# Attention and a two-layer block on one core: the second part of q moves to GpSimd, the factor 0.125 into the exponential, and first-layer units alternate with second-layer units

## The chip, the cores and the metric

The kernel runs on one core of a Trainium2 chip. The metric is the time of one execution on the device, in microseconds (us); less is better. The engines named below are TensorE (PE in the profile: matmuls; PEld: its weight loads), VectorE (DVE), ScalarE (ACT), GpSimd (POOL) and SyncE (SP), which issues the DMAs. PSUM is where TensorE writes. Here it has eight banks in use: four for scores (two buffers of two), three that the two layers share, and one for attention times v.

## The reference

```python
# q, k, v: (8, 8, 576, 64); w_in: (512, 2048); w_out: (2048, 512); all float32
scores = (1.0 / np.sqrt(64)) * np.matmul(q, k.transpose(0, 1, 3, 2))
thresh = np.max(scores, axis=-1, keepdims=True) - tau
scores = np.where(scores >= thresh, scores, -1000000000.0)
scores = scores - np.max(scores, axis=-1, keepdims=True)
attn = np.exp(scores)
attn = attn / (np.sum(attn, axis=-1, keepdims=True) + 1e-09)
x = np.matmul(attn, v)            # then heads side by side: (4608, 512)
h = x @ w_in
g = h * (1.0 / (1.0 + np.exp(-h)))
out = (g @ w_out).astype(np.float32)
```

Every row of scores is cut at its maximum less `tau` (0.02) before the softmax. So small errors in a score decide whether an entry counts, and scores need more accuracy than one rounded product gives.

## The kernel before, in words

**Attention.** Work goes in tiles of 128 rows of scores: 288 tiles in all. Batch 0 is passed twice, first in four "low" visits (16 tiles, rows 0 to 255, computed directly in float32) and then in four "high" ones. Each later batch has four visits of a pair of heads, nine tiles each, so 36 tiles to a batch. For one tile, `scores` multiplies q by k into one of two PSUM buffers (L412). To be accurate, k is split into a rounded part `khi` and a rest `klo` (`split_k`), and q is stacked as a rounded part above its rest in `qstack` (`split_q`), so that two matmuls per half give the whole sum. Then follow the row maximum on VectorE (`soft1`, L422, negated), the threshold on VectorE (L425, maximum less tau), the exponential on ScalarE (`soft1b`, L432, with the negated maximum as its bias), the cut and the row sum on VectorE (`soft2`, L441; it reads the scores again and so frees their buffer), the reciprocal (L445, L449), the scaling on ScalarE (`soft2b`, L454), and the split into two float16 parts on GpSimd (`soft3`, L465, L468, L471). Those are transposed by DMA (L481) and multiplied by v (`av`, L496), two heads at once. `av_post` writes x in two float16 parts (L514, L515).

**q and 0.125.** In batch 0 `split_q` first scales q by `gate` (0.125, or 0 where tau is negative) on ScalarE (L309), rounds it into `qstack` (L310), and GpSimd subtracts to get the rest (L311). From batch 1 on, ScalarE scales and rounds in one step (L315), and VectorE makes the rest, scaling again (L316). `scale_direct` (L349) scales q for the low visits.

**The two layers.** x is taken in chunks of 256 and 320 columns for batch 0 and of 288 for the others, two chunks to a batch. A first-layer unit (`h_unit`, 16 to a chunk) is 12 matmuls into one bank (L530), followed by a chain: tanh on ScalarE (L538), a product on VectorE (L539), the rounded float16 part on ScalarE (L546), its rest on VectorE (L547), into a ring `gbuf` of 17 places. A second-layer unit (`o_unit`) is a quarter of one of four output tiles, 12 matmuls (L562); after the fourth quarter ScalarE evacuates the bank (L572) and SyncE writes it out. `moe_units` gives the 16 first-layer units of a chunk and then its 16 second-layer units. The three banks are handed out in turn by `bank`.

**Weights.** They arrive as 64-bit words. GpSimd, VectorE and ScalarE decode and split them during batch 0 (lines 168 to 214).

**What sets the order.** The program text runs one loop over tiles and drops units between them, at a rate that lets a batch's units end with the next batch. The text's order is a priority only. A scheduler, which reorders the instructions when the program is built, then sets a fixed order for each engine, with scores 1600 places ahead and the steps of the softmax and of `av` ahead by other offsets. On the chip each engine takes its instructions in that order.

## Time and profile before

| | |
|---|---|
| time, three runs | 1277.15, 1279.8 (median), 1281.62 us |
| span of the profiled execution, first to last instruction | 1276.2 us |
| mean granted TensorE clock | 0.969 |
| TensorE busy | 1152.4 us (90%), 9400 matmuls |
| VectorE busy | 967.7 us (76%) |
| ScalarE busy | 819.6 us (64%) |
| GpSimd busy | 751.1 us (59%) |
| chain that ended last | PE 52%, DVE 25%, ACT 6%, DMA 5%, issue 5%, POOL 5% |

The profile gives the span of the profiled execution and no other time of it; the median of the runs is 3.6 us longer than that span. In a row that groups instructions stand the line, the engine, the operation, the tiles it writes and reads, their shapes and the count; then the busy time in us and the mean duration in ns; then the idle time of the engine just before them and what ended it. Tile names stand without their numbers. The rows of stretches of time give for each engine its busy us and, in brackets, its instructions, then the granted clock, the busy share of the DMA engines, and GB/s.

### The profile page before, as it was taken

The numbers are of one execution on the slowest core, as the hardware profiler recorded it, in microseconds if no ns is written. First come the engines' busy times: TensorE is split into PE (matmuls) and PEld (weight loads), VectorE is DVE, ScalarE is ACT, GpSimd is POOL, SyncE is SP. The second block draws the span as 40 slices with busy tenths as digits, with TensorE's granted clock in tenths as the row PEclk, the third lists the DMA queues.
The fourth block names the chain that finished last, engine by engine and source line by source line (L and its number), as shares of the span: only waits on it lengthen the run. The fifth ranks groups of instructions, "written<-read, shape, count | busy, mean of one in ns | idle before, by whom it ended". The sixth has DMA issues, their size and how long they took to land.

```text
span 1276.2 us, 27018 instructions
## 1 busy us (share of the span) xinstructions
PE 1152.4 (90%) x9400; PEld 898.8 (70%) x9400; DVE 967.7 (76%) x2627; ACT 819.6 (64%) x1505; POOL 751.1 (59%) x952
## 2 busy tenths in 40 slices
PE   5774768898899998998989999998999999999998
PEld 3453657676678776776767777786777777777777
DVE  7899998987988989888688858977598848521431
ACT  5787776765867867777476747866477746532431
POOL 4568977787678777874568608781478508300000
PEclk8886989998999999999989999999999999999999
DMA  9457768688778787873768538781687418300000
GB/s 301 121 183 179 172 119 163 138 151 168 135 151 154 135 168 161 156 146 79 152 122 157 114 85 158 148 156 39 129 159 144 103 24 140 72 15 18 8 15 19
DMA packets 363480, 158.15 MB, mean 124 GB/s; under 512 B 329552, under 2 KB 338256, under 8 KB 363344
## 3 DMA queue, kind: packets, MB, share of 16 engines
q1 hardware_dynamic: 363344, 156.43, 59.0%
q8 instruction: 74, 1.21, 0.4%
q14 instruction: 62, 0.51, 0.1%
HBM read 66.72 MB, written 9.44 MB: 60 GB/s over the span
## 4 chain that ended last, share of the span: by engine, by line
PE 52%; DVE 25%; ACT 6%; DMA 5%; issue 5%; POOL 5%; SPq 1%; POOLq 0%; ACTq 0%; DVEq 0%
PE o L562 22%; PE h L530 15%; PE a L496 7%; PE s L412 7%; DVE w L441 6%; DVE sm L422 5%; DVE qstack L316 4%; DMA wT<-hl 3%; ACT w L432 2%; DVE h L539 2%; DVE gbuf L547 2%; POOL hl L468 1%; DMA vraw<-in_vL 1%; ACT w L454 1%; POOL hl L465 1%
## 5 line engine op out<-in xcount | busy, mean ns | idle before, releaser
L530 PE MATMUL h<-x,wst 128*128 128x288 f16 (+2 forms) x3072 | 416.9, 291 | 23.1 <-DVE gbuf L547 19.4
L562 PE MATMUL o<-gbuf,wst 128*128 128x288 f16 (+2 forms) x3072 | 397.3, 287 | 2.5 <-DVE gbuf L547 1.4
L530 PEld LDWEIGHTS <-wst 128*128 128x128 f16 x3072 | 295.0, 99 | 114.9 <-issue 32.0
L562 PEld LDWEIGHTS <-wst 128*128 128x128 f16 x3072 | 291.9, 98 | 85.5 <-issue 8.3
L468 POOL TENSOR_TENSOR hl<-w,hl 128x512 f16<-128x512 f32 x272 | 328.1, 1206 | 15.9 <-ACT hl L463 2.1
L465 POOL TENSOR_SCALAR hl<-w 128x576 f16<-128x576 f32 x264 | 181.5, 690 | 236.6 <-ACT w L454 133.0
L432 ACT ACTIVATE w<-s,sm 128x576 f32<-128x576 f32 x288 | 211.2, 738 | 106.5 <-DVE sm L422 32.2
L441 DVE SCALAR_TENSOR_TENSOR w<-s,sm,w 128x576 f32<-128x576 f32 x288 | 232.7, 812 | 51.1 <-ACT w L432 49.1
L454 ACT ACTIVATE w<-w,sm 128x576 f32<-128x576 f32 x288 | 219.5, 772 | 68.7 <-DVE sm L449 59.5
L422 DVE TENSOR_REDUCE sm<-s 128x1 f32<-128x576 f32 x288 | 216.0, 751 | 55.4 <-PE s L412 51.8
L412 PE MATMUL s<-khi,qstack 128*128 128x288 f32 x608 | 158.7, 342 | 37.2 <-DVE w L441 29.9
L539 DVE SCALAR_TENSOR_TENSOR h<-th,h 128x288 f32<-128x288 f32 (+2 forms) x256 | 116.6, 456 | 80.9 <-ACT th L538 75.8
L538 ACT ACTIVATE th<-h,msc 128x288 f32<-128x288 f32 (+2 forms) x256 | 127.1, 500 | 30.7 <-PE h L530 27.7
L496 PE MATMUL a<-wT,v 128*64 128x288 f16 (+1 forms) x1680 | 131.8, 297 | 14.4 <-DMA wT<-hl 14.1
L546 ACT ACTIVATE gbuf<-h 128x288 f16<-128x288 f32 (+2 forms) x256 | 104.0, 408 | 63.5 <-DVE h L539 62.9
L547 DVE SCALAR_TENSOR_TENSOR gbuf<-h,gbuf 128x288 f16<-128x288 f32 (+2 forms) x256 | 115.0, 452 | 37.9 <-ACT gbuf L546 36.4
L412 PEld LDWEIGHTS s<-khi,qstack 128*128 128x128 f32 x608 | 96.8, 194 | 64.3 <-issue 39.7
L412 PE MATMUL s<-klo,qstack 128*128 128x288 f32 x608 | 133.1, 300 | 0.0
L326 POOL TENSOR_TENSOR klo<-kraw,khi 128x576 fp32r<-128x576 f32 x64 | 93.0, 1453 | 53.9 <-ACT khi L324 52.4
L496 PEld LDWEIGHTS <-v 128*64 128x64 f16 x1680 | 93.7, 112 | 42.1 <-issue 33.3
L412 PEld LDWEIGHTS s<-klo,qstack 128*128 128x128 f32 x608 | 100.2, 193 | 1.0 <-issue 0.2
L471 POOL TENSOR_TENSOR hl<-w,hl 128x64 f16<-128x64 f32 x272 | 94.0, 345 | 0.0
(84 smaller groups left out, 876.5 us busy)
## 6 DMA issues: line engine op xcount, KB each, us to landing
qraw<-in_qT SPq DMA_DIRECT2D x128, 144.0 KB, 3.0
kraw<-in_kT SPq DMA_DIRECT2D x128, 144.0 KB, 3.0
vraw<-in_vL SPq DMA_DIRECT2D x32, 320.0 KB, 3.8
wraw<-in_w_out SPq DMA_DIRECT2D x16, 512.0 KB, 3.9
out_t<-wst SPq DMA_DIRECT2D x56, 144.0 KB, 2.4
wT<-hl SPq DMA_TRANSPOSE x304, 3.4
gbuf<-in_w_in SPq DMA_DIRECT2D x8, 512.0 KB, 7.9
wraw<-in_w_in SPq DMA_DIRECT2D x8, 512.0 KB, 5.4
```

The source lines that it names most:

```text
L412: nc.tensor.matmul(s_ps[:, j, :HALF], lhs, kk[:, j * HALF : (j + 1) * HALF], start=(n == 0), stop=(n == len(seq) - 1),)
L422: nc.vector.tensor_reduce(out=negm, in_=s_ps[:, :, :HALF], op=ALU.max, axis=AX.XY, negate=True)
L432: nc.scalar.activation(wtile[t].rearrange("p (j c) -> p j c", j=2), sps[t][:, :, :HALF], AF.Exp, bias=small[t][:, 0:1],)
L441: nc.vector.scalar_tensor_tensor(out=w3, in0=s_ps[:, :, :HALF], scalar=sm[:, 1:2], in1=w3, op0=ALU.is_ge, op1=ALU.mult, accum_out=sm[:, 2:3],)
L454: nc.scalar.activation(w, w, AF.Copy, scale=r)
L465: nc.gpsimd.tensor_scalar(out=fl[:, 0:S], in0=w, scalar1=1.0, scalar2=1.0, op0=ALU.mult, op1=ALU.mult)
L468: nc.gpsimd.tensor_tensor(out=fl[:, 640:1152], in0=w[:, 0:512], in1=fl[:, 0:512], op=ALU.subtract)
L496: nc.tensor.matmul(a_ps[odd * D : (odd + 1) * D, :n], vt[:, lo_v, odd, kv, :], wT[v, b * H + 2 * p + odd][:, kw, c0 - base : c0 - base + n ...
L530: nc.tensor.matmul(ph[:, :n], wi(c, f, lo_w), x16[b, lo_x][:, c, c0 : c0 + n], start=(k == 0), stop=(k == 11),)
L539: nc.vector.scalar_tensor_tensor(out=ph[:, :n], in0=th[:, :n], scalar=1.0, in1=ph[:, :n], op0=ALU.add, op1=ALU.mult,)
L547: nc.vector.scalar_tensor_tensor(out=g[:, 1, :n], in0=ph[:, :n], scalar=2.0**-14, in1=g[:, 0, :n], op0=ALU.mult, op1=ALU.subtract,)
L562: nc.tensor.matmul(ps[:, :n], wo(f, d, lo_w), g[:, lo_g, :n], start=(f == 0 and k == 0), stop=(f == NF - 1 and k == 2),)
```

## The change

There are three edits. First, q is no longer scaled: ScalarE only rounds it, GpSimd makes the rest for all heads, and `scale_direct` is gone. The factor goes into the exponential as its scale. The exponential's bias must then be the negated maximum times `gate`, and the threshold is the maximum less eight times tau. Both come from one VectorE instruction on two columns, with the constants `cmul` (gate, -1) and `cadd` (0, -8 tau). Second, from batch 1 on the first-layer units of a chunk alternate with the second-layer units of the chunk before it, and the last chunk's second-layer units come at the end. Third, as this needs two whole chunks of g, `gbuf` is larger and addressed by chunk, paid for with a smaller scratch space for DMA descriptors; the first layer takes banks 0 and 1, the second layer bank 2.

```diff
@@ constants
-GB = 17
+GWORDS = 2 * NF * S
@@ def attention_moe
-    gbuf = const.tile([P, GB * 2 * WID], F16, name="gbuf")
+    gbuf = const.tile([P, GWORDS], F16, name="gbuf")
-    gate = const.tile([P, 1], F32, name="gate")
+    cmul = const.tile([P, 2], F32, name="cmul")
+    nc.vector.memset(cmul, -1.0)
+    gate = cmul[:, 0:1]
...
+    cadd = const.tile([P, 2], F32, name="cadd")
+    nc.vector.memset(cadd, 0.0)
...
-        out=ntau, in0=tau_sb, scalar1=0.0, scalar2=-1.0, op0=ALU.max, op1=ALU.mult
+        out=ntau, in0=tau_sb, scalar1=0.0, scalar2=-8.0, op0=ALU.max, op1=ALU.mult
     )
+    nc.vector.tensor_tensor(out=cadd[:, 1:2], in0=ntau, in1=ungated, op=ALU.add)
@@ def pow2_scales
-            allp = bank([P, P], f"{name}_ps")
+            allp = bank([P, P], f"{name}_ps", 0 if turn[1] == 3 else None)
@@ def split_q
-        if h < H:
-            nc.scalar.activation(src, src, AF.Copy, scale=gate)
-            nc.scalar.activation(dst, src, AF.Copy)
-            nc.gpsimd.tensor_tensor(
-                out=dst[D:P, :], in0=src[D:P, :], in1=dst[D:P, :].bitcast(F32), op=ALU.subtract
-            )
-        else:
-            nc.scalar.activation(dst, src, AF.Copy, scale=gate)
-            nc.vector.scalar_tensor_tensor(
-                out=dst[D:P, :], in0=src[D:P, :], scalar=gate[D:P, :],
-                in1=dst[D:P, :].bitcast(F32), op0=ALU.mult, op1=ALU.subtract,
-            )
+        nc.scalar.activation(dst, src, AF.Copy)
+        nc.gpsimd.tensor_tensor(
+            out=dst[D:P, :], in0=src[D:P, :], in1=dst[D:P, :].bitcast(F32), op=ALU.subtract
+        )
@@ def soft1, soft1b
-        nc.vector.tensor_scalar(
-            out=sm[:, 1:2], in0=negm, scalar1=-1.0, scalar2=ntau, op0=ALU.mult, op1=ALU.add
+        nc.vector.scalar_tensor_tensor(
+            out=sm[:, 1:3], in0=cmul, scalar=negm, in1=cadd, op0=ALU.mult, op1=ALU.add
         )
...
-            bias=small[t][:, 0:1],
+            bias=small[t][:, 1:2], scale=gate,
@@ the two layers
+    def place_g(b, c0, n):
+        if gnext[0] + 2 * NF * n > GWORDS:
+            gnext[0] = 0
+        gbase[b, c0] = gnext[0]
+        gnext[0] += 2 * NF * n
...
+    def h_units(b, c0, n, owns=(None,)):
+        return [
+            lambda f=f: h_unit(b, c0, n, f, owns[f % len(owns)]) for f in range(NF)
+        ]
+
+    def o_units(b, c0, n, own=None):
+        return [
+            lambda d=d, quarter=quarter: o_unit(b, c0, n, d, quarter, own)
+            for d in range(DM // P) for quarter in range(4)
+        ]
+
+    held = []
+
     def moe_units(b, c0, n):
-        for f in range(NF):
-            yield lambda f=f: h_unit(b, c0, n, f)
-        for d in range(DM // P):
-            for quarter in range(4):
-                yield lambda d=d, quarter=quarter: o_unit(b, c0, n, d, quarter)
+        if b == 0:
+            return h_units(b, c0, n) + o_units(b, c0, n)
+        out = []
+        if held:
+            for pair in zip(h_units(b, c0, n, (0, 1)), o_units(*held.pop(), 2)):
+                out.extend(pair)
+        else:
+            out = h_units(b, c0, n)
+        held.append((b, c0, n))
+        return out
@@ the loop over tiles
+        if held and not ready and not units and t >= NT + 8:
+            units.extend(o_units(*held.pop()))
@@ def kernel
-    nc = bacc.Bacc("TRN2", target_bir_lowering=False, num_devices=1)
+    nc = bacc.Bacc(
+        "TRN2", target_bir_lowering=False, num_devices=1, dynamic_dma_scratch_size=1024
+    )
```

Since a scheduler decides the order, here is what it made of both programs at three places. Names carry their numbers: `s_192` are the scores of tile slot 192, `h_3_288_1` is first-layer unit 1 of the chunk of batch 3 that begins at column 288, `o_3_0_1` is output tile 1 of the chunk at column 0, and a last number is the buffer's. The changed kernel's lines are a few lower or higher than before: L422, L425, L441, L445, L539, L547 are now L418, L421, L437, L441, L544, L551.

VectorE around tile 192, before:

```order
L422 TENSOR_REDUCE sm_193_9891<-s_193_9843 128x1
L449 RECIPROCAL sm_191_9774<-sm_191_9774 128x1
L316 SCALAR_TENSOR_TENSOR qstack1_87<-qraw_24_41_9855,gate_79,qstack1_87 64x576
L425 TENSOR_SCALAR sm_192_9839<-sm_192_9839,ntau_81 128x1
L547 SCALAR_TENSOR_TENSOR gbuf_61<-h_3_0_9_8459,gbuf_61 128x288
L425 TENSOR_SCALAR sm_193_9891<-sm_193_9891,ntau_81 128x1
L547 SCALAR_TENSOR_TENSOR gbuf_61<-h_3_0_10_8496,gbuf_61 128x288
L441 SCALAR_TENSOR_TENSOR w32_192_9840,sm_192_9839<-s_192_9778,sm_192_9839,w32_192_9840 128x576
```

and of the change:

```order
L418 TENSOR_REDUCE sm_192_9578<-s_192_9528 128x1
L551 SCALAR_TENSOR_TENSOR gbuf_61<-h_3_288_1_9029,gbuf_61 128x288
L421 SCALAR_TENSOR_TENSOR sm_191_9524<-cmul_79,sm_191_9524,cadd_82 128x2
L421 SCALAR_TENSOR_TENSOR sm_192_9578<-cmul_79,sm_192_9578,cadd_82 128x2
L437 SCALAR_TENSOR_TENSOR w32_191_9525,sm_191_9524<-s_191_9472,sm_191_9524,w32_191_9525 128x576
L437 SCALAR_TENSOR_TENSOR w32_192_9579,sm_192_9578<-s_192_9528,sm_192_9578,w32_192_9579 128x576
L441 TENSOR_SCALAR sm_191_9524<-sm_191_9524 128x1
L544 SCALAR_TENSOR_TENSOR h_3_288_2_9084<-th_3_288_2_9125,h_3_288_2_9084 128x288
```

The rest of q (L316) has left VectorE's row. The two small instructions of a pair of tiles still stand between the reduces and the cuts, but they are two-tensor instructions now and follow one another.

GpSimd at the head that is loaded for the same place, before:

```order
L471 TENSOR_TENSOR hl_189_9732<-w32_189_9663,hl_189_9732 128x64
L326 TENSOR_TENSOR klo_41_9941<-kraw_24_41_9856,khi_41_9939 128x576
L465 TENSOR_SCALAR hl_190_9785<-w32_190_9722 128x576
L468 TENSOR_TENSOR hl_190_9785<-w32_190_9722,hl_190_9785 128x512
L471 TENSOR_TENSOR hl_190_9785<-w32_190_9722,hl_190_9785 128x64
```

and of the change:

```order
L461 TENSOR_SCALAR hl_190_9535<-w32_190_9469 128x576
L327 TENSOR_TENSOR klo_41_9701<-kraw_24_41_9595,khi_41_9699 128x576
L318 TENSOR_TENSOR qstack1_93<-qraw_24_41_9594,qstack1_93 64x576
L464 TENSOR_TENSOR hl_190_9535<-w32_190_9469,hl_190_9535 128x512
L467 TENSOR_TENSOR hl_190_9535<-w32_190_9469,hl_190_9535 128x64
```

The rest of q stands right behind the rest of k, ahead of the two float16 subtractions of tile 190.

TensorE where one first-layer unit ends, before:

```order
L530 MATMUL h_2_288_7_7311<-x16_2_1_4317,wst_89 128x288
L530 LDWEIGHTS wst_89
L530 MATMUL h_2_288_7_7311<-x16_2_0_4316,wst_89 128x288
L530 LDWEIGHTS wst_89
L530 MATMUL h_2_288_8_7332<-x16_2_0_4316,wst_89 128x288
```

and of the change:

```order
L535 MATMUL h_3_288_7_9435<-x16_3_1_6164,wst_95 128x288
L535 LDWEIGHTS wst_95
L535 MATMUL h_3_288_7_9435<-x16_3_0_6163,wst_95 128x288
L566 LDWEIGHTS wst_95
L566 MATMUL o_3_0_1_9221<-gbuf_61,wst_95 128x288
```

Unit 7 was followed by unit 8; now it is followed by twelve matmuls of the second layer and then by unit 8.

More of the change, by code (lines that the diff above doesn't have):

```diff
@@ L90, in attention_moe @@
     )
+    cadd = const.tile([P, 2], F32, name="cadd")
+    nc.vector.memset(cadd, 0.0)
+    ungated = const.tile([P, 1], F32, name="ungated")
+    nc.vector.tensor_scalar(
+        out=ungated, in0=tau_sb, scalar1=0.0, scalar2=-3.0e38, op0=ALU.is_lt, op1=ALU.mult
+    )
     ntau = const.tile([P, 1], F32, name="ntau")
     nc.vector.tensor_scalar(
-        out=ntau, in0=tau_sb, scalar1=0.0, scalar2=-1.0, op0=ALU.max, op1=ALU.mult
+        out=ntau, in0=tau_sb, scalar1=0.0, scalar2=-8.0, op0=ALU.max, op1=ALU.mult
     )
+    nc.vector.tensor_tensor(out=cadd[:, 1:2], in0=ntau, in1=ungated, op=ALU.add)
     qstack = []
@@ L344, in load_direct @@
         direct[v] = qt, kt
-    def scale_direct(v):
-        for j in range(2):
-            own = direct[v][0][j * D : (j + 1) * D, 256 * j : 256 * (j + 1)]
-            nc.scalar.activation(own, own, AF.Copy, scale=gate[j * D : (j + 1) * D, :])
     def soft3_direct(t):
@@ L418, in soft1 @@
         s_ps = sps[t]
-        sm = sb.tile([P, 5], F32, tag="small", name=f"sm_{t}", bufs=4)
+        sm = sb.tile([P, 6], F32, tag="small", name=f"sm_{t}", bufs=4)
         w = sb.tile([P, S], F32, tag="w32", name=f"w32_{t}", bufs=4)
@@ L441, in soft2 @@
         nc.vector.scalar_tensor_tensor(
-            out=w3, in0=s_ps[:, :, :HALF], scalar=sm[:, 1:2], in1=w3,
-            op0=ALU.is_ge, op1=ALU.mult, accum_out=sm[:, 2:3],
+            out=w3, in0=s_ps[:, :, :HALF], scalar=sm[:, 2:3], in1=w3,
+            op0=ALU.is_ge, op1=ALU.mult, accum_out=sm[:, 3:4],
         )
         nc.vector.tensor_scalar(
-            out=sm[:, 3:4], in0=sm[:, 2:3], scalar1=1e-9, scalar2=2.0**-12,
+            out=sm[:, 4:5], in0=sm[:, 3:4], scalar1=1e-9, scalar2=2.0**-12,
             op0=ALU.add, op1=ALU.mult,
         )
-        nc.vector.reciprocal(out=sm[:, 4:5], in_=sm[:, 3:4])
+        nc.vector.reciprocal(out=sm[:, 5:6], in_=sm[:, 4:5])
     def soft2b(t):
         w = wtile[t]
-        r = small.pop(t)[:, 4:5]
+        r = small.pop(t)[:, 5:6]
         nc.scalar.activation(w, w, AF.Copy, scale=r)
@@ L521, in attention_moe, with h_unit @@
     gt = {}
-    gcount = [0]
+    gbase = {}
+    gnext = [0]
     po = {}
-    def h_unit(b, c0, n, f):
-        ph = bank([P, 512], f"h_{b}_{c0}_{f}")
+    def place_g(b, c0, n):
[3 more added lines that the diff above has]
+        gnext[0] += 2 * NF * n
+    def h_unit(b, c0, n, f, own=None):
+        if f == 0:
+            place_g(b, c0, n)
+        ph = bank([P, 512], f"h_{b}_{c0}_{f}", own)
         k = 0
@@ L553, in h_unit, with o_unit @@
         return post
-    def o_unit(b, c0, n, d, quarter):
+    def o_unit(b, c0, n, d, quarter, own=None):
         if quarter == 0:
-            po[b, c0, d] = bank([P, 512], f"o_{b}_{c0}_{d}")
+            po[b, c0, d] = bank([P, 512], f"o_{b}_{c0}_{d}", own)
         ps = po[b, c0, d]
@@ L695, in attention_moe @@
     t = 0
-    while t < NT + 8 or units or ready:
+    while t < NT + 8 or units or ready or held:
         while ready and ready[0][0] <= t:
```

7 lines of the change are left out of this document (3 added, 4 removed).

## The prediction

> **What bounds the kernel now.** I read first the busy time by stretch, cut where the work changes: weights and batch 0, then batch 1, then the steady batches, then what is left when no scores are.
>
> ```profile
> core 0: us, PE busy (x) PEld busy (x) DVE busy (x) ACT busy (x) POOL busy (x), PEclk, DMA share, GB/s
> 0.00:227.00 227.00, 157.95 (x1086) 117.09 (x1088) 206.14 (x497) 165.56 (x301) 160.09 (x174) 0.88 0.70 178
> 227.00:382.00 155.00, 139.32 (x1120) 107.14 (x1116) 135.27 (x391) 111.30 (x197) 117.46 (x153) 0.97 0.75 145
> 382.00:1093.00 711.00, 676.17 (x5721) 532.50 (x5720) 571.65 (x1618) 481.38 (x877) 467.31 (x617) 0.99 0.66 129
> 1093.00:1276.20 183.20, 178.92 (x1483) 142.08 (x1480) 54.63 (x125) 61.41 (x134) 6.24 (x10) 1.00 0.08 21
> ```
>
> VectorE sets the pace of stage 1 (206.1 of 227 us, 91%). In stage 2 it has 87%. In stage 3 TensorE is the bound (676.2 of 711 us) with 34.8 us of idle, and VectorE has 80%. Stage 4 is TensorE alone: only a shorter matmul could shorten it, and the change has none. Then I asked what TensorE waited for in stages 2 and 3 (total, times, longest):
>
> ```profile
> PE s L412 <- DVE w L441: 23.8, 15, 3.8
> PE h L530 <- DVE gbuf L547: 10.7, 14, 1.7
> PE a L496 <- DMA wT<-hl: 7.3, 8, 1.8
> PE s L412 <- DVE sm L425: 2.6, 4, 1.0
> PE o L562 <- DVE gbuf L547: 1.4, 1, 1.4
> ```
>
> Scores wait for VectorE to free their PSUM buffer (23.8 and 2.6 us). First-layer units wait for the last step of an earlier unit's chain, which frees the bank (10.7; 1.4 is a second-layer unit's). These are the waits that the two halves of the change can touch. Durations come from the groups of instructions (busy us, mean ns of one):
>
> ```profile
> L422 DVE TENSOR_REDUCE sm<-s 128x1 f32<-128x576 f32 x288 | 216.0, 751 | 55.4 <-PE s L412 51.8 <-PE s L400 2.6
> L432 ACT ACTIVATE w<-s,sm 128x576 f32<-128x576 f32 x288 | 211.2, 738 | 106.5 <-DVE sm L422 32.2 <-DVE sm L445 31.0 <-POOL hl L471 28.1
> L441 DVE SCALAR_TENSOR_TENSOR w<-s,sm,w 128x576 f32<-128x576 f32 x288 | 232.7, 812 | 51.1 <-ACT w L432 49.1
> L425 DVE TENSOR_SCALAR sm<-sm,ntau 128x1 f32<-128x1 f32 x288 | 59.2, 209 | 2.2
> L267 DVE SCALAR_TENSOR_TENSOR msc<-msc,o_w_sc 128x1 f32<-128x1 f32 x8 | 4.5, 561 | 0.0
> L257 DVE TENSOR_TENSOR msc<-v_sc,i_w_sc 128x1 f32<-128x1 f32 x8 | 4.0, 495 | 0.0
> L316 DVE SCALAR_TENSOR_TENSOR qstack<-qraw,gate,qstack 64x576 fp32r<-64x576 f32 x56 | 73.3, 1309 | 4.3 <-ACT qstack L315 2.4
> L326 POOL TENSOR_TENSOR klo<-kraw,khi 128x576 fp32r<-128x576 f32 x64 | 93.0, 1453 | 53.9 <-ACT khi L324 52.4
> L311 POOL TENSOR_TENSOR qstack<-qraw,qstack 64x320 fp32r<-64x320 f32 x8 | 7.6, 954 | 0.6
> ```
>
> **The small instruction of every tile.** L425 (209 ns, one SBUF tensor and two scalars) becomes a scalar_tensor_tensor of 128x2 with two SBUF tensors. The nearest rows are L267, the same operation on one element, and L257, also of two SBUF tensors. Their means are 561 and 495 ns, though one element is no work. The instructions of these two lines, min/median/max in ns, tell more:
>
> ```profile
> L267 DVE SCALAR_TENSOR_TENSOR msc<-msc,o_w_sc x8: 143/523/1010, 158.9 to 1072.9; 128x1 f32<-128x1 f32 x8
> L425 DVE TENSOR_SCALAR sm<-sm,ntau x288: 196/209/217, 12.6 to 1094.6; 128x1 f32<-128x1 f32 x144
> ```
>
> L425 never strays; L267 goes from 143 to 1010. One of the long ones in the timeline (start, us) shows why:
>
> ```profile
> 783.64 1.16 POOL L468 TENSOR_TENSOR hl<-w,hl 128x512 f16<-128x512 f32 x1
> 783.81 1.00 DVE L267 SCALAR_TENSOR_TENSOR msc<-msc,o_w_sc 128x1 f32<-128x1 f32 x1
> 784.74 0.81 DVE L441 SCALAR_TENSOR_TENSOR w<-s,sm,w 128x576 f32<-128x576 f32 x1
> ```
>
> It starts inside a GpSimd instruction (783.64 to 784.80) and ends with it (784.81). So I read the wait as one for GpSimd's current instruction. The new one takes 143 ns at least and some 1010 at most; I take 561, so +0.352 us per tile, because GpSimd is as busy where it will stand.
>
> [...]
>
> Tiles and removed L316 by stage are counted with these rows (us of VectorE, times), first the reduces, one per tile:
>
> ```profile
> 0.00:227.00 227.00, 35.76 (x48) 0.88 0.70 178
> 227.00:382.00 155.00, 36.11 (x48) 0.97 0.75 145
> 382.00:1093.00 711.00, 143.56 (x192) 0.99 0.66 129
> ```
>
> then L316:
>
> ```profile
> 0.00:227.00 227.00, 5.20 (x4) 0.88 0.70 178
> 227.00:382.00 155.00, 13.21 (x11) 0.97 0.75 145
> 382.00:1093.00 711.00, 54.91 (x41) 0.99 0.66 129
> ```
>
> *Stage 1:* 48 × 0.352 = +16.9, less 5.2, is +11.7 us of VectorE. It was 91% busy, so I let four fifths through: **+9 us**. At the bounds: 48 × (0.143 − 0.209) − 5.2 = −8, and 48 × 0.80 − 5.2 = +33.
> *Stage 2:* +16.9 − 13.2 = +3.7, taken as **+3**; bounds −16 and +25.
> *Stage 3:* 192 × 0.352 = +67.6, less 54.9, is +12.7: VectorE goes from 571.7 to 584 of 711 us and is still not the bound. But the place changes too. L425 ran beside the exponential. The new one stands before it, since the exponential takes its bias. Tiles go in pairs: two reduces, one exponential that nothing covers and two L441 are 0.75 + 0.75 + 0.74 + 0.81 + 0.81 = 3.9 us, and two new instructions of 0.56 make it 5.0, before the scores and the hops between engines. A pair has 711/96 = 7.4 us. So on average it fits; where tiles come quicker, it does not.
>
> **The second part of q.** 56 L316 leave VectorE, each up to 1309 ns in the middle of the tiles' queue. GpSimd gets 56 subtractions of 64x576. L326 has the same columns (1453 ns); scaling L311 by columns gives 954 × 576/320 = 1717. I take 1.45: +81 us on GpSimd, 59 in stage 3. [...] That is hidden as long as the transposes behind it are early: av waited 7.3 us for them. Behind each new subtraction queue the parts of w (L465, L468, L471), then SP's transposes, then av. The scores of the next head wait for it too, as they waited for L316.
>
> **0.125 in the exponential.** The eight L309 and L349 leave ScalarE. It was at 165.6 of 227 us in stage 1, so VectorE covers that: 0. The start gains nothing either:
>
> ```profile
> 4.37 1.28 ACT L349 ACT_TABLE_LOAD   x1 [4.37 <-DMA gbuf<-in_qT]
> 6.23 4.21 PE L400 MATMUL s<-kd,gbuf 128*128 128x288 f32 x8 [6.23 <-ACT gbuf L349]
> 10.44 0.82 DVE L239 TENSOR_REDUCE vmx<-vraw 128x1 f32<-128x640 f32 x1 [1.26 <-DMA vraw<-in_vL]
> 11.17 1.41 DVE L422 TENSOR_REDUCE sm<-s 128x1 f32<-128x576 f32 x2
> ```
>
> The first scores could start up to 1.9 us sooner (6.23 to 4.37), but the first reduce of them waited behind v's reduces, which waited for DMA.
>
> **Alternation.** These are the rows of a first-layer unit's matmuls and of the second layer's evacuation:
>
> ```profile
> L530 PE MATMUL h<-x,wst 128*128 128x288 f16 (+2 forms) x3072 | 416.9, 291 | 23.1 <-DVE gbuf L547 19.4 <-DVE sm L445 1.2 <-DVE x L515 1.1
> L572 ACT ACTIVATE wst<-o,msc 128x288 f32<-128x288 f32 (+2 forms) x64 | 31.5, 494 | 84.3 <-PE o L562 84.2
> ```
>
> No matmul is added. A first-layer unit is 12 matmuls, 12 × 416.9/3072 = 1.6 us. Now mostly 12 or more second-layer matmuls stand before the next, so a bank's chain has about twice the time. I take the waits of 10.7 and 1.4 us as gone but for one: **−11**. The first layer's elementwise work also spreads over the whole batch, and that with the missing L316 should take some of the 26.4 us that scores wait, while the longer chain gives some back: net **−9**. Stage 3 is then −20, out of 34.8 at most. At its other bound the whole 67.6 lies on the path, less 11: +57.
>
> Three costs of this part I put at 0, each with its cover. The second layer has one bank now, so a unit's first matmul waits for L572 (494 ns, and 738 more if an exponential is ahead of it on ScalarE, 1.23 us in all). The first-layer unit of 1.6 us that mostly stands between covers this. Without it, the 47 changes of output tile before the last scores cost up to 1.23 us each, 58 us. Second, the x of a batch is read until the batch's last first-layer unit, some 16 units or 26 us later than now. Its space is next written two batches on, each of 36 × 711/192 = 133 us. Third, the v maximum's matmul always takes bank 0, eight times in all. The new gbuf holds two whole chunks, so a unit writes where second-layer units two chunks back have read. Stage 4 is 0, as in both orders 119 of 512 units follow the last scores, and none of its 183.2 us is spent on elementwise work that TensorE waits for.
>
> **Sum:** 0 + 9 + 3 − 20 + 0 = −8 on the span of 1276.2, so 1268.2. The median of the runs, 1279.8, is 3.6 over that span; with it **1272 us**.
>
> **Rivals.**
> *Slower: the tile chain pays for GpSimd.* Where two of the new instructions follow each other, the first lets GpSimd's next instruction queue and the second waits for all of it. If half the tiles of stage 3 pay on TensorE's path, that is 33.8 − 11 = +23; with +11.7 and +3.7 unhidden, +38: 1318. It decides once a pair's chain outlasts the matmuls between its scores. For it: 143 to 1010 ns, and 91% in stage 1. Against it: the 7.4 us per pair.
> [...]
> *More gain: the small instruction is not held.* At 209 ns only the loss of L316 is left: four fifths of 5.2 in stage 1, −4; half of 13.2 in stage 2, where TensorE idles 15.7 us, −6. In stage 3 the bank waits go and 15 of the 26.4 us, −26. Sum −36: 1244. Against it stands the mean of L267; for it, its minimum of 143.
> *GpSimd becomes the bound.* If half of the 59 us in stage 3 reaches av, −8 + 30 = +22: 1302. [...]
> *Nothing:* L316's 73 us out and the new waits in cancel on VectorE's queue, stage 1 costs what the banks give (+9 and −11), and the scores' waits stay: 1278 to 1282.
> *The change does not do what it says:* a scheduler sets the order, and if it ran the second-layer units in blocks again the −11 would be gone and 1283 the result. In the new order they do alternate, if loosely (12 to 44 second-layer matmuls between two units), so I give this no chance of its own.
>
> **Chances.** Forecast 0.44, of which 0.34 comes out below 1276 and 0.10 within; more gain 0.12; nothing 0.08; tile chain 0.28; GpSimd 0.08. What this kernel can tell from no change is 0.3%, 3.8 us. So faster 0.46, same 0.18, slower 0.36. The range goes from 1242 to 1315: it leaves out nearly half of the tile-chain rival, the far end of the gain and little else. The forecast's own range is 1254 to 1284: stage 1 between 0 and +15, stage 3 between −29 and −14, the rest as it is.
>
> **What would show it.** The new small instruction: mean near 0.56 us with a minimum near 0.15 (right), or near 0.2 (more gain). TensorE's waits for gbuf: 1 or 2 us. Scores' waits for L441's successor: under 20 us right, over 45 the first rival. VectorE's busy time: 968 + 101 − 73 = 996. GpSimd's: above 832, with av's wait for transposes unchanged unless it is the bound. Stage 1 should end about 9 us later. What would make it wrong is an order of the scores set tighter than the chain really is: a static order cannot fill such a gap with other units.

## The result and the profile after

The changed kernel takes 1292.4 us (median of four runs, 1288.2 to 1295.8), against 1279.0 us (1277.2 to 1281.6) for the kernel before, run beside it. The ratio is 1.0109, with a 95% interval of 1.0074 to 1.0144: slower, by about 13 us. The forecast was 1272 us and faster; the time lies within the range of 1242 to 1315, on the wrong side of no change.

Busy time by stretch of the changed kernel, cut at the same tiles as the prediction's rows of before (the starts of tiles 48 and 96, and the last reduce):

```profile
core 0: us, PE busy (x) PEld busy (x) DVE busy (x) ACT busy (x) POOL busy (x), PEclk, DMA share, GB/s
0.00:236.40 236.40, 163.77 (x1079) 121.12 (x1080) 214.52 (x499) 163.70 (x284) 161.19 (x178) 0.85 0.66 172
236.40:412.10 175.70, 149.63 (x1174) 115.31 (x1172) 144.74 (x391) 119.96 (x208) 131.38 (x167) 0.90 0.67 129
412.10:1109.90 697.80, 670.39 (x5674) 531.19 (x5673) 587.11 (x1574) 494.29 (x873) 517.29 (x656) 0.99 0.64 130
1109.90:1291.80 181.90, 178.19 (x1479) 141.81 (x1477) 51.02 (x116) 57.55 (x126) 5.62 (x9) 1.00 0.08 21
```

Set against before, whose rows for exactly these tiles follow, the four stages changed by +9.0, +20.8, -12.7 and -1.5 us, which is the +15.6 between the two spans (1276.2 and 1291.8).

```profile
0.00:227.40 227.40, 158.35 (x1092) 117.46 (x1094) 206.54 (x498) 165.78 (x301) 160.09 (x174) 0.88 0.70 178
227.40:382.30 154.90, 139.22 (x1116) 106.91 (x1114) 134.87 (x389) 111.37 (x197) 117.76 (x153) 0.97 0.75 145
382.30:1092.80 710.50, 675.67 (x5716) 532.21 (x5717) 571.46 (x1617) 480.88 (x875) 466.81 (x617) 0.99 0.66 128
1092.80:1276.20 183.40, 179.12 (x1484) 142.23 (x1482) 54.82 (x125) 61.61 (x134) 6.44 (x10) 1.00 0.08 21
```

The stretches do not hold equal work: in stage 2 TensorE now has 58 more matmuls (1174 for 1116), which at 139.22/1116 = 0.125 us are some 7 of the 20.8 us and were taken from the other stages. Idle time, 26.1 us for 15.7, is 10.4 of it, so some 3 us are left, at a granted clock of 0.90 for 0.97. Stage 3 gave up 42 matmuls (5674 for 5716), some 5 of its 12.7 us; its idle time fell by 7.4 us, from 34.8 to 27.4. Over the whole span TensorE is idle 6.0 us longer (span less busy: 129.8 for 123.8) and busy 9.6 us longer (1162.0 for 1152.4) with the same 9400 matmuls, at a mean granted clock of 0.951 for 0.969.

What TensorE waited for in stages 2 and 3 of the changed kernel (236.4 to 1109.9 us), as the prediction read it for before (total us, times, longest):

```profile
PE s L408 <- DVE w L437: 24.1, 16, 4.0
PE h L535 <- DVE gbuf L551: 13.0, 9, 3.7
PE a L492 <- DMA wT<-hl: 7.0, 6, 3.0
PE o L566 <- ACT wst L576: 5.6, 7, 1.5
```

The waits of first-layer units for their bank, which the prediction saw gone, have grown from 10.7 to 13.0 us, and the scores wait 24.1 us for VectorE's L437, where it was 23.8. (Over the whole span it is 23.4 for 19.4 and 30.6 for 29.9.) In the steady stage alone it looks different; these are the waits there, of the changed kernel and then of before:

```profile
PE h L535 <- DVE gbuf L551: 9.8, 6, 3.7
PE s L408 <- DVE w L437: 9.7, 10, 2.1
PE o L566 <- ACT wst L576: 5.6, 7, 1.5
```

```profile
PE s L412 <- DVE w L441: 17.7, 12, 2.4
PE h L530 <- DVE gbuf L547: 9.2, 11, 1.7
PE s L412 <- DVE sm L425: 2.6, 4, 1.0
```

The scores' waits fell there by some 11 us, as forecast, but rose in stage 2, from 6.1 to 14.6; the bank waits stayed; the second layer's single bank added 5.6. The groups of instructions that the change touched:

```profile
L421 DVE SCALAR_TENSOR_TENSOR sm<-cmul,sm,cadd 128x2 f32<-128x2 f32 x288 | 165.0, 579 | 2.1
L428 ACT ACTIVATE w<-s,sm,cmul 128x576 f32<-128x576 f32 x288 | 236.5, 830 | 140.5 <-DVE sm L421 108.1
L318 POOL TENSOR_TENSOR qstack<-qraw,qstack 64x576 fp32r<-64x576 f32 (+1 forms) x64 | 88.4, 1381 | 4.9
```

The small instruction takes 579 ns (forecast 561) and the subtraction on GpSimd 1381 (forecast 1450). What was not forecast is the exponential: 830 ns in place of 738. It also sat waiting for the small instruction for 108.1 us.

Stage 2 shows best what the loss looks like. Here are three pieces of it of the changed kernel, then the same of before (stretch, length, then busy us and instructions of the engines, and the granted clock):

```profile
305.00:320.00 15.00, 9.20 (x59) 6.89 (x56) 13.61 (x34) 8.03 (x13) 8.63 (x11) 0.82 0.67 151
320.00:335.00 15.00, 7.41 (x37) 5.81 (x37) 11.44 (x33) 10.01 (x14) 14.83 (x22) 0.50 0.75 128
335.00:350.00 15.00, 10.93 (x71) 8.33 (x69) 11.21 (x25) 8.33 (x14) 10.60 (x14) 0.77 0.65 129
```

```profile
305.00:320.00 15.00, 10.41 (x75) 8.07 (x74) 10.32 (x31) 8.77 (x14) 11.21 (x16) 0.77 0.74 147
320.00:335.00 15.00, 11.19 (x83) 8.43 (x78) 14.90 (x41) 12.44 (x24) 9.36 (x13) 0.89 0.74 140
335.00:350.00 15.00, 13.45 (x113) 10.40 (x112) 13.49 (x42) 11.78 (x23) 11.01 (x16) 1.00 0.73 131
```

TensorE's rows there, in order of time, show what it had to do (start, us):

```profile
318.21 0.68 PE L408 MATMUL s<-klo,qstack 128*128 128x288 f32 x2
322.10 0.82 PE L408 MATMUL s<-khi,qstack 128*128 128x288 f32 x2 [3.20 <-DVE w L437]
...
327.22 0.82 PE L408 MATMUL s<-khi,qstack 128*128 128x288 f32 x2 [2.44 <-DVE w L437]
...
332.45 2.61 PE L492 MATMUL a<-wT,v 128*64 128x288 f16 x20 [2.97 <-DMA wT<-hl]
```

No unit of either layer stands in this piece: scores wait for the tile chain to free their buffer, then attention times v (L492) waits for its transposes, and TensorE runs at half its clock (0.50) through the 15 us, beside waits of 3.2, 2.4 and 3.0 us. What lowers the clock, no run here shows. The hold that the prediction described (a VectorE instruction that ends only with GpSimd's) stands in the same place, on VectorE and then on GpSimd:

```profile
319.75 0.88 DVE L421 SCALAR_TENSOR_TENSOR sm<-cmul,sm,cadd 128x2 f32<-128x2 f32 x1
```

```profile
319.21 1.40 POOL L327 TENSOR_TENSOR klo<-kraw,khi 128x576 fp32r<-128x576 f32 x1 [4.28 <-DMA wT<-hl]
```

The small instruction starts within GpSimd's (319.21 to 320.61) and ends with it, at 320.63. This single hold did not make the wait of 3.20 us. Those scores waited for the cut of the tile before (VectorE, L437, from 321.12), whose own small instruction was done at 318.99. Its exponential began only at 320.28, behind L325, L317 and L450 on ScalarE. So the piece shows TensorE starved, and what causes it has to come from the experiments.

### The profile page after: what moved, and what is told of

It reads as the page before. It is cut to its first block, busy times and chain, and to the rows that moved or that the text cites. A ratio compares the mean times of both kernels' runs of the same rounds, so it can differ in the third digit from the quotient of the medians.

```text
span 1291.8 us, 26873 instructions
## 1 busy us (share of the span) xinstructions
PE 1162.0 (90%) x9400; PEld 909.4 (70%) x9400; DVE 997.4 (77%) x2575; ACT 835.5 (65%) x1489; POOL 815.5 (63%) x1008
## 4 chain that ended last, share of the span: by engine, by line
PE 47%; DVE 29%; ACT 9%; DMA 6%; POOL 4%; issue 4%; SPq 0%; ACTq 0%; POOLq 0%; DVEq 0%
PE o L566 18%; PE h L535 16%; PE s L408 6%; DVE w L437 6%; DVE sm L418 6%; PE a L492 6%; DVE sm L421 5%; ACT w L428 3%; DMA wT<-hl 3%; ACT w L450 2%; DMA vraw<-in_vL 2%; DVE gbuf L551 2%; DVE h L544 2%; DVE wst L221 2%; DVE v L286 1%
## 5 line engine op out<-in xcount | busy, mean ns | idle before, releaser
L535 PE MATMUL h<-x,wst 128*128 128x288 f16 (+2 forms) x3072 | 433.9, 291 | 29.6 <-DVE gbuf L551 23.4
L566 PE MATMUL o<-gbuf,wst 128*128 128x288 f16 (+2 forms) x3072 | 428.2, 290 | 6.8 <-ACT wst L576 5.6
L464 POOL TENSOR_TENSOR hl<-w,hl 128x512 f16<-128x512 f32 x272 | 320.0, 1176 | 14.0 <-ACT hl L459 2.1
L428 ACT ACTIVATE w<-s,sm,cmul 128x576 f32<-128x576 f32 x288 | 236.5, 830 | 140.5 <-DVE sm L421 108.1
L461 POOL TENSOR_SCALAR hl<-w 128x576 f16<-128x576 f32 x264 | 177.8, 678 | 190.7 <-ACT w L450 157.1
L437 DVE SCALAR_TENSOR_TENSOR w<-s,sm,w 128x576 f32<-128x576 f32 x288 | 232.1, 811 | 44.7 <-ACT w L428 42.6
L450 ACT ACTIVATE w<-w,sm 128x576 f32<-128x576 f32 x288 | 217.6, 770 | 55.6 <-DVE sm L445 52.1
L418 DVE TENSOR_REDUCE sm<-s 128x1 f32<-128x576 f32 x288 | 214.4, 749 | 49.0 <-PE s L408 46.6
L544 DVE SCALAR_TENSOR_TENSOR h<-th,h 128x288 f32<-128x288 f32 (+2 forms) x256 | 115.8, 454 | 103.6 <-ACT th L543 101.8
L408 PE MATMUL s<-khi,qstack 128*128 128x288 f32 x608 | 159.8, 344 | 31.8 <-DVE w L437 30.6
L421 DVE SCALAR_TENSOR_TENSOR sm<-cmul,sm,cadd 128x2 f32<-128x2 f32 x288 | 165.0, 579 | 2.1
L551 DVE SCALAR_TENSOR_TENSOR gbuf<-h,gbuf 128x288 f16<-128x288 f32 (+2 forms) x256 | 114.9, 450 | 42.4 <-ACT gbuf L550 41.9
L492 PE MATMUL a<-wT,v 128*64 128x288 f16 (+1 forms) x1680 | 132.5, 301 | 11.7 <-DMA wT<-hl 11.5
L492 PEld LDWEIGHTS <-v 128*64 128x64 f16 x1680 | 96.0, 114 | 38.0 <-issue 22.3
```

Source lines behind the costliest of these rows:

```text
L408: nc.tensor.matmul(s_ps[:, j, :HALF], lhs, kk[:, j * HALF : (j + 1) * HALF], start=(n == 0), stop=(n == len(seq) - 1),)
L418: nc.vector.tensor_reduce(out=negm, in_=s_ps[:, :, :HALF], op=ALU.max, axis=AX.XY, negate=True)
L421: nc.vector.scalar_tensor_tensor(out=sm[:, 1:3], in0=cmul, scalar=negm, in1=cadd, op0=ALU.mult, op1=ALU.add)
L428: nc.scalar.activation(wtile[t].rearrange("p (j c) -> p j c", j=2), sps[t][:, :, :HALF], AF.Exp, bias=small[t][:, 1:2], scale=gate,)
L437: nc.vector.scalar_tensor_tensor(out=w3, in0=s_ps[:, :, :HALF], scalar=sm[:, 2:3], in1=w3, op0=ALU.is_ge, op1=ALU.mult, accum_out=sm[:, 3:4],)
L450: nc.scalar.activation(w, w, AF.Copy, scale=r)
```

## Experiments

Fourteen kernels were run, each against the kernel before. This table holds them all: the ratio to before with its 95% interval, and of the profiled execution the span and TensorE's busy and idle time (span less busy). The kernel before, run again beside each, had medians from 1275.9 to 1279.2 us.

| run | median us | ratio | span | PE busy | PE idle |
|---|---|---|---|---|---|
| before | 1279.0 | 1 | 1276.2 | 1152.4 | 123.8 |
| the change | 1292.4 | 1.0109 [1.0074, 1.0144] | 1291.8 | 1162.0 | 129.8 |
| alternate_only | 1245.7 | 0.9756 [0.9726, 0.9787] | 1244.2 | 1142.3 | 101.9 |
| q_and_exp_only | 1292.3 | 1.0110 [1.0074, 1.0145] | 1285.3 | 1151.8 | 133.5 |
| blocks_large_gbuf | 1276.3 | 1.0000 [0.9985, 1.0014] | 1276.7 | 1152.5 | 124.2 |
| two_scalars | 1262.7 | 0.9885 [0.9853, 0.9917] | 1258.1 | 1143.1 | 115.0 |
| scale_as_number | 1279.0 | 1.0017 [1.0000, 1.0035] | 1275.7 | 1152.6 | 123.1 |
| two_scalars_number | 1241.1 | 0.9709 [0.9694, 0.9725] | 1237.9 | 1141.6 | 96.3 |
| repaired_in_blocks | 1266.1 | 0.9915 [0.9888, 0.9942] | 1264.8 | 1150.7 | 114.1 |
| alternate_q_gpsimd | 1263.7 | 0.9883 [0.9860, 0.9907] | 1257.5 | 1142.6 | 114.9 |
| q_rest_on_vector | 1300.2 | 1.0157 [1.0119, 1.0195] | 1289.2 | 1157.1 | 132.1 |
| small_twice | 1314.9 | 1.0280 [1.0259, 1.0302] | 1316.2 | 1166.5 | 149.7 |
| held_beside_exp | 1307.3 | 1.0244 [1.0223, 1.0266] | 1307.5 | 1160.3 | 147.2 |
| held_before_exp | 1306.9 | 1.0249 [1.0211, 1.0286] | 1312.8 | 1159.2 | 153.6 |
| plain_beside_exp | 1259.3 | 0.9855 [0.9803, 0.9907] | 1258.6 | 1146.6 | 112.0 |
| plain_four_more | 1280.2 | 1.0022 [1.0006, 1.0038] | 1279.8 | 1157.4 | 122.4 |

### Each half of the change alone

alternate_only is the kernel before with the second and third edits alone (order, `gbuf`, banks, scratch space); q_and_exp_only is it with the first alone, units in blocks.

```diff
 alternate_only, soft1:                    as before
+    for pair in zip(h_units(b, c0, n, (0, 1)), o_units(*held.pop(), 2)): ...
 q_and_exp_only, moe_units:                as before
+    nc.vector.scalar_tensor_tensor(out=sm[:, 1:3], in0=cmul, scalar=negm, in1=cadd, ...)
+    bias=small[t][:, 1:2], scale=gate
```

> The kernel before with the alternation alone (larger gbuf, banks by layer, units held one chunk); q, threshold and exponential as before. GpSimd theory (the two-tensor small instruction waits for GpSimd on every tile's chain and that is what the change loses): the small instruction stays at 0.21 us, tiles 0 to 96 take about 382 us as before instead of 412, tiles 168 to 276 gain what they gained in the changed kernel (434 to about 405 us), and the time is 1250 to 1265 us. Rival (the new order of the units loses the time, since batch 1 starts with first-layer units alone and the second layer has one bank): tiles 48 to 108 stay near 219 us as in the changed kernel (191 before), and the time is 1285 us or more.

> The kernel before with q's second part on GpSimd, 0.125 in the exponential and the two-tensor small instruction; the units in blocks as before. GpSimd theory: small instruction 0.55 to 0.6 us, exponential 0.83 us, tiles 0 to 96 take 405 to 420 us, and as tiles come close together in blocks, stage 3 pays too: 1300 to 1325 us. Rival (order of units): close to before, 1275 to 1285 us.

The alternation alone gains 2.4%, 31 us by the ratio, more than either expectation. The other half alone loses 1.1%, between its two expectations, and with it the alternation adds nothing: 1292.3 without and 1292.4 with it. So the two do not add up. TensorE's waits of alternate_only in its steady stage (383 to 1060 us) are the ones that the prediction had hoped for:

```profile
PE o L570 <- ACT wst L580: 7.4, 5, 3.1
PE s L412 <- DVE w L441: 2.9, 4, 1.8
PE h L539 <- DVE gbuf L555: 2.1, 2, 1.4
```

Bank waits went from 9.2 to 2.1 us and scores' waits from 21.3 (17.7, 2.6 and 1.0 for L449) to 3.9. So the step on the alternation was right in mechanism, and it is the q half that undoes it. The waits are not the whole gain, though: stage 3 is 34.0 us shorter than before (676.5 for 710.5), of which 20.4 are idle time, and the other 13.6 are less busy time of TensorE for nearly the same matmuls (5697 for 5716), which no run here explains.

### Is it the order, or the memory that came with it?

blocks_large_gbuf keeps the alternation's larger `gbuf` and smaller scratch space, but gives the units in blocks, with the banks in turn.

```diff
-        if b == 0:
+        if b < B:
             return h_units(b, c0, n) + o_units(b, c0, n)
```

> The kernel before with only the larger gbuf, its addressing by chunk and the smaller scratch space; units in blocks and banks in turn. If the alternation itself gives the 31 us of alternate_only: 1272 to 1282 us. If the larger gbuf gives them (first-layer units no longer wait for a place among 17): 1245 to 1260 us.

1.0000: the memory gives nothing. The gain is that of the order, together with the banks handed out by layer; no run separates those two.

### Which part of the q half costs

Three kernels mend the change. two_scalars gives the small work as two instructions with one SBUF tensor each. scale_as_number gives the exponential 0.125 as a number in place of the column `gate`, and two_scalars_number does both, with the factor of its first small instruction as a number too; these two leave out the case of a negative tau.

```diff
 two_scalars
-        nc.vector.scalar_tensor_tensor(
-            out=sm[:, 1:3], in0=cmul, scalar=negm, in1=cadd, op0=ALU.mult, op1=ALU.add
+        nc.vector.tensor_scalar(
+            out=sm[:, 1:2], in0=negm, scalar1=gate, scalar2=None, op0=ALU.mult
+        )
+        nc.vector.tensor_scalar(
+            out=sm[:, 2:3], in0=negm, scalar1=-1.0, scalar2=cadd[:, 1:2], op0=ALU.mult, op1=ALU.add
         )
 scale_as_number
-            bias=small[t][:, 1:2], scale=gate,
+            bias=small[t][:, 1:2], scale=0.125,
 two_scalars_number: both of these, and against two_scalars
-            out=sm[:, 1:2], in0=negm, scalar1=gate, scalar2=None, op0=ALU.mult
+            out=sm[:, 1:2], in0=negm, scalar1=0.125, scalar2=None, op0=ALU.mult
```

> The changed kernel with the small two-tensor instruction as two instructions of one tensor (negated maximum times gate; negated maximum times -1 plus the threshold's offset). GpSimd theory: each takes about 0.2 us with no spread, VectorE's busy time falls by some 45 us to about 950, ScalarE's wait for it falls from 108 us to under 50, tiles 0 to 96 take about 390 us, and the time is 1262 to 1275 us. Rival (order of units): 1285 to 1292 us. Rival (slower exponential, 738 to 830 ns): 1285 us or more, since the exponential is as long as in the changed kernel.

> The changed kernel with the exponential's scale as the number 0.125 instead of a column read from SBUF; leaves out the case of a negative tau. Rival (slower exponential): it returns from 0.83 to 0.74 us, ScalarE's busy time falls by 26 us, and if the exponential lies on the chain of the tiles the time is 1265 to 1278 us. GpSimd theory: the exponential gets shorter but the small instruction keeps its 0.58 us, the time falls by 5 to 12 us to 1280 to 1287 us.

> The changed kernel with both repairs: two one-tensor small instructions and the exponential's scale (and the bias's factor) as the number 0.125; leaves out the case of a negative tau. If the two costs add as they were measured one by one (30 and 13 us): 1245 to 1255 us, tiles 0 to 168 in about 638 us against 667. If they lie on the same chain and only the longer one counts: 1258 to 1264 us.

The small instruction's form is worth 30 us (1292.4 to 1262.7), the column 13 (to 1279.0, between its two expectations), and both together 51 (to 1241.1), 8 more than their sum and below both expectations. Some of the 8 can come from the further difference of that kernel: without the column the first small instruction takes 146 ns for 207, some 18 us of VectorE in all. The groups of two_scalars_number:

```profile
L431 ACT ACTIVATE w<-s,sm 128x576 f32<-128x576 f32 x288 | 207.9, 737 | 90.1 <-DVE sm L424 57.6 <-DVE sm L448 13.6 <-DVE sm L421 9.3
L424 DVE TENSOR_SCALAR sm<-sm,cadd 128x1 f32<-128x1 f32 x288 | 57.5, 202 | 0.0
L421 DVE TENSOR_SCALAR sm<-sm 128x1 f32<-128x1 f32 x288 | 41.9, 146 | 1.0
```

Two instructions of 146 and 202 ns (207 and 202 in two_scalars) take less than one of 579. Stage 2, cut at the same tiles, shows each cost: 175.7 us in the change, 161.0 without the hold (two_scalars), 170.2 without the column (scale_as_number), 155.4 without either, and 154.9 before. In the steady stage of two_scalars_number (391 to 1052 us) the bank waits are down to 1.9 us and the scores' waits for L440 to 0.8, as in alternate_only. With both costs gone the change is a gain of 2.9%, the fastest kernel of this study; with a negative tau kept, alternate_only is, at 2.4%.

repaired_in_blocks takes the alternation out of it again (the same case left out):

```diff
-        if b == 0:
+        if b < B:
```

> two_scalars_number (both repairs) with the units in blocks and the banks in turn; leaves out the case of a negative tau. If the alternation's 31 us add to those of the repaired q part: 1268 to 1276 us. If both take the same idle time of TensorE in tiles 96 to 276: 1245 to 1260 us.

1266.1, between the two expectations: there the alternation is worth 25 us, nearly the 31 it is worth on the kernel before. Even mended, the q half adds only 0.5% to the alternation (0.9756 to 0.9709).

### Is it GpSimd's new subtractions?

Two tries follow. alternate_q_gpsimd is alternate_only with every head's q made as batch 0's is (scaled and rounded on ScalarE, the rest on GpSimd). q_rest_on_vector is the change with the rest of q by VectorE from batch 1 on.

```diff
 alternate_q_gpsimd
-        if h < H:
+        if h < B * H:
 q_rest_on_vector
-        nc.gpsimd.tensor_tensor(
+        eng = nc.gpsimd if h < H else nc.vector
+        eng.tensor_tensor(
```

> Alternation with q's second part on GpSimd for all heads, in batch 0's way (ScalarE scales q in place, rounds it, GpSimd subtracts), with exponential and threshold as before. Theory (the exponential's part is what costs; q on GpSimd is worth what it takes from VectorE): ScalarE gets some 37 us more, VectorE 73 us less, tiles 168 to 276 take 385 to 400 us, and the time is 1230 to 1248 us. Rival (GpSimd's 81 us more delay the transposes and the heads): tiles 0 to 168 slow down as in the changed kernel (616 to about 640 us or more) and the time is 1262 us or more.

> The changed kernel with the second part of q on VectorE again from batch 1 on (a subtraction of two tensors), so alternation and the exponential's part without GpSimd's 56 subtractions. Theory (exponential's part costs): tiles 0 to 168 stay at 650 us or more, VectorE's busy time is about 1060 us, and the time is 1285 to 1320 us. Rival (GpSimd's load costs): the small instruction waits less, GpSimd returns to about 755 us and the time is 1250 to 1270 us.

The first settles nothing. It came out 18 us slower than alternate_only, but ScalarE now stands in its own queue before q has landed:

```profile
L309 ACT ACTIVATE qraw<-qraw,gate 128x576 f32<-128x576 f32 (+1 forms) x64 | 47.8, 748 | 83.5 <-DMA qraw<-in_qT 80.4 <-POOL hl L471 3.1
```

83.5 us of waiting and 56 added instructions there are a cost of their own. In the second GpSimd is back at 758.6 us busy without the 56 subtractions, and the time is 1300.2, 8 us more and not less. But they now cost VectorE 47 us (1044.8 for 997.4), so this run alone does not say what they cost on GpSimd. two_scalars_number does: it keeps them there (821.4 us busy) and is the fastest kernel of all. The subtractions on GpSimd are not the loss.

### How the small instruction costs: three theories

My first theory was the prediction's chain: the exponential takes its bias from the held instruction and waits (108.1 us of ScalarE). Its rival: it costs VectorE's time, wherever it stands. small_twice gives it a second time in the changed kernel, result unused. held_beside_exp gives alternate_only's small instruction the two-tensor form, with the exponential still taking its bias from the reduce; held_before_exp is the same with the bias from the held instruction.

```diff
 small_twice, on the change
+        nc.vector.scalar_tensor_tensor(
+            out=twin, in0=cmul, scalar=negm, in1=cadd, op0=ALU.mult, op1=ALU.add
+        )
 held_beside_exp, on alternate_only
-        nc.vector.tensor_scalar(
-            out=sm[:, 1:2], in0=negm, scalar1=-1.0, scalar2=ntau, op0=ALU.mult, op1=ALU.add
+        nc.vector.scalar_tensor_tensor(
+            out=sm[:, 1:3], in0=cmul, scalar=negm, in1=cadd, op0=ALU.mult, op1=ALU.add
         )
 held_before_exp, on held_beside_exp
-            bias=small[t][:, 0:1],
+            bias=small[t][:, 1:2],
```

> The changed kernel with the two-tensor small instruction done twice per tile, the second result unused. GpSimd theory: the twin costs VectorE about 0.6 us too (the second of two waits for GpSimd's next instruction), VectorE's busy time goes to some 1160 us, tiles 0 to 168 grow by about 0.4 to 0.6 us each, 70 to 100 us, the later ones by less, and the time is 1360 to 1440 us. Rival (the small instruction is off the path): 1290 to 1305 us.

> Alternation alone, but with the small instruction of every tile as the two-tensor form (it waits for GpSimd); only the threshold comes from it, the exponential still takes its bias from the reduce, and stays at 0.74 us. Theory (what costs is the time between reduce and exponential, not VectorE's time): VectorE has some 100 us more than with the alternation alone, small_twice showed 23 us for 128 us of that kind, so 1255 to 1270 us. Rival (VectorE's time costs, wherever the instruction stands): the same as held_before_exp within 6 us.

> The same instructions as held_beside_exp, but the exponential takes its bias (a copy of the negated maximum) from the two-tensor instruction and so waits for it. Theory: ScalarE waits some 100 us in all for it, tiles 0 to 168 take about 645 us (616 with the alternation alone), and the time is 1275 to 1290 us, 15 us or more above held_beside_exp. Rival: within 6 us of held_beside_exp.

small_twice cost 23 us, between its two expectations, for 94 us more of VectorE (1090.9 busy for 997.4): 0.24 us per us. The other two cost 62 and 61 us over alternate_only, and do not differ from each other, though only in the second does ScalarE wait for the small instruction. The small instruction's row of held_beside_exp, then the exponential's of held_before_exp:

```profile
L432 DVE SCALAR_TENSOR_TENSOR sm<-cmul,sm,cadd 128x2 f32<-128x2 f32 x288 | 163.5, 573 | 1.9
```

```profile
L439 ACT ACTIVATE w<-s,sm 128x576 f32<-128x576 f32 x288 | 212.0, 739 | 184.8 <-DVE sm L432 92.0 <-DVE sm L456 43.1 <-DVE sm L452 32.9
```

So the theory of the exponential's wait falls: 92.0 us of such waits cost nothing that could be measured. What both have in common is a held instruction on VectorE's queue, 94 to 96 us more busy (1055.4 and 1057.0 for 961.5), at 0.65 us per us.

Is that VectorE's time as such? Two last runs put unheld time in the same place: alternate_only with its one-tensor small instruction given two and four times more, results unused.

```diff
+        nc.vector.tensor_scalar(
+            out=sm[:, 5:6], in0=negm, scalar1=-1.0, scalar2=ntau, op0=ALU.mult, op1=ALU.add
+        )        # and again, two or four in all
```

> The alternation alone, with the small instruction of every tile given twice more in its one-tensor form (results unused), beside the exponential: about 0.41 us more of VectorE per tile, 118 us in all, nothing of it held by GpSimd. held_beside_exp put 94 us more on VectorE at the same place, held, and cost 61 us (0.65 us per us). If that price is VectorE's time as such, this run costs 0.65 x 118 = 77 us over alternate_only: about 1322 us, and 1300 at the least. If the price lies in the hold (its long ones, up to over 1 us, which the fixed order does not allow for), evenly spread time that the order allows for costs no more than the second instruction of small_twice did (0.24 us per us): 1245 to 1275 us. Between 1275 and 1300 both share.

> As plain_beside_exp, with the one-tensor instruction given four times more in place of twice. In plain_beside_exp two more raised VectorE's busy time by only 58.5 us (961.5 to 1020.0), since one begins before the last has ended, and cost 13.6 us over alternate_only (0.23 us per us). Four more should raise it by some 117 us, more than the 94 of held_beside_exp. If each us of VectorE costs the same, held or not, and only the amount was too small, this run costs 0.65 x 117 = 76 us, 1322 us, and at least the 61 us of held_beside_exp, 1307. If unheld time stays at 0.23 us per us, it costs 27 us: 1273, and surely under 1290.

Two more came to 1259.3, 13.6 us over alternate_only. They overlap, so that VectorE's busy time rose by 58.5 us only and not by 118, and the run alone was not enough. Four more put 111 us on VectorE, more than the held one did, and cost 34 us (0.9756 to 1.0022; 0.31 us per us) against 61. The two engines' busy times of plain_four_more and then of held_beside_exp:

```profile
PE 1157.4 (90%) x9400; PEld 903.5 (71%) x9400; DVE 1072.9 (84%) x3779; ACT 819.4 (64%) x1505; POOL 760.2 (59%) x952
```

```profile
PE 1160.3 (89%) x9400; PEld 901.6 (69%) x9400; DVE 1055.4 (81%) x2631; ACT 815.8 (62%) x1505; POOL 758.9 (58%) x952
```

VectorE has more to do in the first and TensorE is idle 122.4 us, in the second 147.2. So in these kernels VectorE's time has a price, and a held microsecond has about twice that price. At 0.31 the 94 us would be 29 of the 61; by this subtraction the other 32 go with the hold. Its instructions go from 194 to 2843 ns in held_beside_exp (median 506), where the unheld ones all take about 0.2 us; a fixed order has to take each delay as it comes. Whether the unevenness does the harm, or that the order was made without knowing of it, these runs do not tell apart. Nor do they say why a second held instruction beside the first cost only 0.24.

## Why the prediction was wrong, by its own steps

**Bounds.** Stage 4 hardly moved (-1.5 us), as read, and VectorE's work came out at 997.4 us against 996.

**Small instruction.** 579 ns against 561; its minimum was 202 ns, not 143. Its size was right, and so was the cause: of the 245 that have a row of their own in the changed kernel's timeline, 170 took over 0.30 us, and 166 of these end within 0.04 us of the end of a GpSimd instruction. The bound of some 1010 ns at most was too low, as a hold can outlast GpSimd's current instruction: the longest took 1634 ns.

**Stage 1**, +9: it came out at +9.0, but the agreement does not confirm the reckoning. With neither hold nor column stage 1 still lasts 236.3 us (two_scalars_number) for 236.4 in the change. The hold alone, put on alternate_only, does add 9.4 (held_beside_exp, 235.2 for 225.8). What else in the q half lengthens this stage stays open, so the figure was met in part by luck.

**Stage 2**, +3: this is the step that failed. It came out at +20.8, within its bounds of -16 and +25, near the bad one. I reckoned it by VectorE's busy time (+3.7 us of work; the trace has 144.74 for 134.87, partly work moved there). But stage 2 has a piece in which no unit fills the waits between scores, so that delays of the tile chain come through to TensorE. The 0.37 us more per tile (579 ns for 209) were let through as if they were averaged over the stage. The runs show the two costs that made the loss: without the hold stage 2 is 14.7 us shorter (two_scalars), without the column 5.5 (scale_as_number), and without either it is back at 155.4. The hold alone, put on alternate_only, adds 13.3 there (held_beside_exp, 170.9 for 157.6), and q_and_exp_only has the loss with units in blocks (171.2). The halved clock is a small part: two_scalars_number and q_and_exp_only are both granted 0.92 in stage 2, and only one of them is longer than before.

**Stage 3**, -20: it came out at -12.7. Some 5 of that is work that stage 2 took over. The scores' part was right in this stage (-9 forecast; 21.3 to 10.0); over stages 2 and 3 together, from which the 26.4 us were read, it was not, as stage 2 took most of it back. The bank waits, -11, did not go: 9.2 and now 9.8. alternate_only and two_scalars_number show that they do go (2.1 and 1.9) when VectorE's small instructions are not held, so the mechanism was right and the cover was taken away by the other edit; I had costed the two as if they were independent. The second layer's single bank, put at 0, cost 5.6.

These misses, +17.8, +7.3 and -1.5, are the 23.6 us between the 1268.2 forecast for the span and the 1291.8 measured.

**0.125 in the exponential**, 0: wrong, and the trace of before had the row. I counted ScalarE's eight instructions that go, not what a scale read as a column adds to each of 288. Two ScalarE rows of before, of one shape, with the column `gate` and without:

```profile
L315 ACT ACTIVATE qstack<-qraw,gate 128x576 fp32r<-128x576 f32 x56 | 42.9, 766 | 2.0 <-PE s L412 2.0
L324 ACT ACTIVATE khi<-kraw 128x576 fp32r<-128x576 f32 x64 | 43.6, 682 | 11.7 <-PE s L412 10.3 <-DMA kraw<-in_kT 0.9
```

84 ns a time. In the exponential it was 92 (738 to 830), 26 us of ScalarE, and taking the column away gave 13 us of time. That ScalarE was 64% busy did not hide it; the likely reason, not tested apart, is that the exponential stands between a tile's reduce and its cut.

**GpSimd**, hidden: right. Its subtractions are not the loss (two_scalars_number), and av's wait for its transposes stayed (7.0 us for 7.3 in stages 2 and 3). Its busy time, named as above 832 us, came to 815.5, as its other instructions took some 16 us less.

**The rivals.** "More gain", 1244 us if the small instruction is not held, has its condition in two_scalars_number, which has neither hold nor column and takes 1241. That the totals agree is luck: its stages 1 to 3 changed by +8.9, +0.5 and -49.4 us, where the rival had -4, -6 and -26. "The tile chain pays for GpSimd", 1318, came nearest in cause, though 26 us too high and with the loss in stage 3 and not in stage 2. Its premise, that the second of two waits for all of GpSimd's next instruction, is seen: in 19 of the 23 places of the changed kernel where two of them stand one right behind the other, the second took 0.34 to 1.46 us and ended with a GpSimd instruction that began within 0.12 us of the first one's end; in the other four it took 0.21 us. Its path is not confirmed: I had it lie between reduce and exponential, and held_beside_exp costs as much with the exponential free. The test named in advance (scores' waits under 20 or over 45) gave 24.1 in stages 2 and 3, in between; the waits for gbuf, named as 1 or 2 us, were 13.7 there.

## What to carry to other kernels

Here a tiny instruction in an in-order queue cost what it waited for, not what it computed: two instructions of 207 and 202 ns with one SBUF tensor each beat one of 579 ns with two, and that choice alone was worth 30 us. Price every operand that an edit turns from a number into a column on each instruction that repeats per tile (here 92 ns on each of 288 exponentials), and look for a row of the same shape with and without it. And test edits alone: here one gained 31 us, the other lost 13, and together the gain was gone. With the hold and the column mended it was there again (25 us), so the second edit had taken away the slack that the first lived on.
